# First layer's input of a two-layer attention and gated-unit kernel: transposes moved from TensorE to transfers, the norm in one ScalarE operation, maxima started later

## The chip, the cores and the metric

The kernel runs on one core of one Trainium2 chip. The metric is the device time of the whole program in microseconds (us), the median of several runs. The core's engines each work through their own instruction stream in order and wait for each other by semaphores: TensorE (PE in the profile, its weight loads PEld), VectorE (DVE), ScalarE (ACT), GpSimd (POOL) and SyncE (SP), which here only issues transfers. A queue is an engine's stream of issued transfers; SPq is that of SyncE.

## The reference

Two layers, each an attention block with one shared key and value head and a gated unit behind it. Sizes: 2048 positions, width 448, 16 query heads of 28, hidden width 1792.

```python
def _A_ref(x, wq, wk, wv, wo):                # x: (1, 2048, 448)
    q = (x @ wq) -> (1, 16, 2048, 28)
    k = x @ wk                                # (1, 2048, 28), one head for all
    v = x @ wv
    p = softmax(q @ k.T * 28 ** -0.5)
    return (p @ v -> (1, 2048, 448)) @ wo
def _B_ref(x, w_gate, w_up, w_down):
    return (sigmoid(x @ w_gate) * (x @ w_up)) @ w_down

for _ in range(2):                            # both layers use the same weights
    x = x + _A_ref(layernorm(x), wq, wk, wv, wo)
    x = x + _B_ref(layernorm(x), w_gate, w_up, w_down)
```

## The kernel before

The positions are cut in 16 tiles of 128 rows. Every matrix product takes its f32 operands as a high and a low f16 part. The program has a start (the input of the first layer), then for each layer a main loop of 16 query tiles times 16 key tiles ("steps"), with the gated unit of earlier tiles and other work filled in between.

**The start.** For each tile of x: load (`load_x0`, SP), statistics on VectorE and the inverse deviation on GpSimd (`s0`, `rstd`, L295 to L300, in groups of two or four tiles), the norm and the split in high and low parts (`s1` with `ln_split` and `hilo`: VectorE subtracts and multiplies, L314; ScalarE casts the high part, L306; GpSimd subtracts for the low part, L307 and L308), seven 128x128 transposes on TensorE and their copy to `XT0` by ScalarE (`s2` with `t7`, L320 and L322), the products with the key and value weights (`s3` with `kv`, L337) and the parts of the keys (`build`, L364 to L370), and two transposes of the keys on TensorE with a copy into `KK` (`s4` with `kvt`, L376 to L380). The tile `hl` that holds high and low parts has two buffers, `ktl` (the keys' parts) two. The four stages run staggered in one loop, tile i - 4 in `s1`, i - 6 in `s2`, i - 7 in `s3`, i - 8 in `s4`. Weights are prepared beside it: `prep_kv`, `prep_q`, and `prep_b` for the output projection (`ro`, `WO`) and the gated unit (`rmax` pieces are loaded and squared for a scale).

Projections of the queries (`qproj`, 16 groups of 11 matmuls, four for each block of 512 queries) are generators that a filler (`fill.slice(ns)`) advances by an estimated time. From iteration `SM` on, `first_mx` also makes one of the 16 groups of maxima for the first query tile (`mx_gen`: four matmuls of queries and keys, L472, and four reductions on VectorE, L476). A softmax step of a tile can only start when all 16 groups of that tile are made, reduced, transposed (`fin`, L491) and written into `QS`.

**The main loop.** For each step the order is written out: `ORDER = "FSFSFSFSPXM"`, four scores with an exp each (S: L502, L505), fill slices between (F: query projections first, then the gated unit), the value products of the step before (P: L513), preparation and stages of earlier tiles (X), one group of maxima of the next query tile (M). `paced` advances `prep_b` by step along `PLAN`; the fill rate is the work left over the steps left, with the query projections due by step 48.

Transfers are issued in program order on their engine, and each takes one of eight semaphores in turn, so an issue waits until the transfer eight places before it has landed.

Of the kernel before, what the change touches and what calls it, by code (L numbers as in the profile page):

```python
# [19 lines left out]
def interleaved_layers_kernel(ctx: ExitStack, tc: tile.TileContext, x, wq, wk, wv, wo, wg, wu, wd, out, layers=2):  # L20
# [134 lines left out]
    def prep_q():  # L155
        parts = wk1.tile([128, 4], F32, name="parts", bufs=1)
        for c in range(4):
            junk = wk1.tile([128, D], F32, tag="P", name="junq", bufs=8)
            squares(parts[:, c:c + 1], rq[:, c], junk)
# [106 lines left out]
    PLAN = [(0, 18), (24, 33), (30, 37), (63, 65), (71, 73)]  # L266
# [26 lines left out]
    def rstd(mv, r, n):  # L293
# [6 lines left out]
        nc.gpsimd.tensor_tensor(w, y, z, op=OP.mult)  # L300
        return [(mv[:, i, 0:1], w[:, i:i + 1]) for i in range(n)]
# [14 lines left out]

    def t7(hl, XT, t, ev=nc.vector.tensor_copy):
        p = fps([128, 7, 128], F16, "t7")
        for c in range(7):
            nc.tensor.transpose(p[:, c], hl[:, c], id16)  # L320
            yield C128
        defer(lambda: ev(XT[:, :, t * 128:(t + 1) * 128], p))  # L322
# [21 lines left out]
    ktl = [cst.tile([128, 8, 32], F16, name=f"ktl{i}") for i in range(2)]  # L344
# [11 lines left out]
    def kv(l, XT, t, kt, start=False):  # L356
# [3 lines left out]
        kt_ = ktl[kt % 2]  # L360

        def build():
            if start:
                nc.scalar.activation(kt_[:, 0, 0:28], p[:, 0:28], AF.Copy, scale=2.0 ** -18)  # L364
            else:
                nc.vector.tensor_scalar(kt_[:, 0, 0:28], p[:, 0:28], 2.0 ** -18, None, op0=OP.mult)
            nc.scalar.activation(VV[l][:, kt, 0:28], p[:, 28:56], AF.Copy, scale=2.0 ** -16)
            nc.vector.scalar_tensor_tensor(kt_[:, 1, 0:28], p[:, 0:28], 2.0 ** -18, kt_[:, 0, 0:28],
                                           op0=OP.mult, op1=OP.subtract)
            nc.vector.tensor_copy(kt_[:, 2:8, 0:28], kt_[:, 0:1, 0:28].to_broadcast([128, 6, 28]))  # L370
        defer(build)

    def kvt(l, kt, ev=nc.vector.tensor_copy):
        p = fps([128, 2, 128], F16, "kvt")
        k = ktl[kt % 2].rearrange("p a d -> p (a d)")
        nc.tensor.transpose(p[:, 0], k[:, 0:128], id16)  # L376
        nc.tensor.transpose(p[:, 1], k[:, 128:256], id16)
        yield 2 * C128

        defer(lambda: ev(KK[l][:, :, kt * 128:(kt + 1) * 128], p))  # L380
# [159 lines left out]
    class Block:  # L540
# [143 lines left out]
        def down(self, t, hs):  # L684
# [35 lines left out]
            def dd():  # L720
                if u == 3:
                    fill.gens.insert(0, [qgen(l + 1, 0), G * QCH])
                yield from kv(l + 1, v["XT"], u % 4, u, True)

            def de():
                kt = u
                nc.sync.dma_start_transpose(KK[l + 1][:, :, kt * 128:(kt + 1) * 128],
                                            ktl[kt % 2].rearrange("p a d -> p (a d)"))
                return
                yield  # L730
# [53 lines left out]
    def load_x0(i):  # L784
        xr0[i] = wk1.tile([128, D], F32, tag="h", name="xr0", bufs=HB)
# [16 lines left out]
    def s0(i):  # L802
# [7 lines left out]
        if i in last:  # L810
            n = i + 1 - mvr["a"]
            for j, t in enumerate(rstd(mvr["m"], mvr["r"], n)):
                ls0[mvr["a"] + j] = t
        return
        yield

    def s1(i):
        hl0[i] = ln_split(xr0[i], *ls0[i], nc.gpsimd, xr0[i], nc.scalar.copy)
        if i + HB < NT:
            load_x0(i + HB)  # L820
        return
        yield

    def s2(i):
        flush()
        yield from t7(hl0[i], XT0[i // 4], i % 4, nc.scalar.copy)
        flush()

    def s3(i):
        yield from kv(0, XT0[i // 4], i % 4, i, True)  # L830
        flush()

    def s4(i):
        yield from kvt(0, i, nc.scalar.copy)
# [145 lines left out]
```

## Time and profile before

| | us |
|---|---|
| median of three runs | 2366.12 (2365.82 to 2366.45) |
| the profiled execution's own time | 2366.16 |
| its span, first to last instruction | 2364.4 |
| first exp of the main loop | 106.80 after the span's start |
| mean granted TensorE clock | 0.985 |

Times in the profile count from the span's start; the profiled execution's own time has 1.76 us around the span. In a row of the timeline stand the start, the duration, the engine, the line, the operation, output <- input, their shapes, the count of merged instructions, and in brackets the idle time before and what ended it. In a row of a stretch stand the busy time and the number of instructions of each engine, the granted clock, the share of the transfer engines and GB/s. Line numbers are those of the kernel before.

### The profile page before, as it was taken

To read this page: it belongs to the slowest core of one execution; us is meant where nothing else is said; L and a number is where in the kernel's file an instruction comes from. 1 tells how busy PE (TensorE), PEld (TensorE's weight loads), DVE (VectorE), ACT (ScalarE), POOL (GpSimd) and SP (SyncE) were. 2 spreads that over 40 slices of the span, in tenths; PEclk is the share of its full clock that TensorE was granted. 3 is DMA by queue.
4 is the path that set the end of the run, shared out by engine and by line. 5 is a ranking of instruction groups with operands and counts; after the bars stand their busy time and mean duration, and the time that the engine had idled before them with its cause. 6 is when DMAs were issued, how large, how long until landed. Compare 5 with 4: busy or idle time off the path is not lost.

```text
span 2364.4 us, 41202 instructions
## 1 busy us (share of the span) xinstructions
PE 2239.7 (95%) x15736; PEld 1002.3 (42%) x15736; DVE 1636.2 (69%) x2909; ACT 1562.9 (66%) x2598; POOL 342.0 (14%) x606
## 2 busy tenths in 40 slices
PE   5798899999999999999998999999999999999999
PEld 2222244444444444444572224444444444444456
DVE  6788787777667777773358877767677777777321
ACT  5587777677667676777413777767676776767751
POOL 5203664001110100101001011000000000000010
PEclk9799999999999999999998999999999999999999
DMA  3333563323223232322342113322231313223133
GB/s 113 108 100 92 183 197 103 91 72 94 86 64 97 78 90 72 94 91 73 99 140 53 27 49 91 87 73 83 65 103 58 96 56 102 76 82 94 57 113 116
DMA packets 208071, 213.88 MB, mean 90 GB/s; under 512 B 139952, under 2 KB 168304, under 8 KB 207872
## 3 DMA queue, kind: packets, MB, share of 16 engines
q1 hardware_dynamic: 202496, 196.36, 28.5%
q0 software_dynamic: 5376, 14.87, 1.8%
q8 instruction: 123, 2.02, 0.4%
q14 instruction: 76, 0.62, 0.1%
HBM read 175.37 MB, written 23.59 MB: 84 GB/s over the span
## 4 chain that ended last, share of the span: by engine, by line
PE 51%; DVE 5%; DMA 1%; ACT 1%; issue 0%; SPq 0%; POOL 0%; ACTq 0%; DVEq 0%; POOLq 0%
PE pv L513 12%; PE s L502 10%; PE dn L694 8%; PE gp L337 7%; PE up L337 7%; DVE mp L476 4%; PE mx L472 4%; PE wo L604 2%; PE qp L337 1%; ACT P L505 0%; DMA sums<-rc 0%; DMA KK<-ktl 0%; DVE st L289 0%; DMA XT<-hl 0%; SPq L582 0%
## 5 line engine op out<-in xcount | busy, mean ns | idle before, releaser
L505 ACT ACTIVATE P<-s,esc 128x512 f32<-128x512 f32 x2048 | 1308.6, 688 | 517.1 <-PE s L502 500.2
L476 DVE TENSOR_REDUCE mp<-mx 128x1 f32<-128x512 f32 x2048 | 1268.2, 682 | 410.1 <-PE mx L472 406.1
L502 PE MATMUL s<-QS,KK 96*128 96x512 f16 x2048 | 762.0, 381 | 53.8 <-DVE mp L476 35.0
L337 PEld LDWEIGHTS <-wgu 128*128 128x128 f16 x4928 | 458.7, 98 | 243.7 <-issue 96.4
L513 PE MATMUL pv<-P,VV 128*32 128x512 f32 x4096 | 547.4, 607 | 0.0
L337 PE MATMUL up<-XT,wgu 128*128 128x256 f16 x2464 | 375.8, 273 | 0.6 <-DVE mp L476 0.6
L337 PE MATMUL gp<-XT,wgu 128*128 128x256 f16 x2464 | 375.2, 274 | 0.2
L694 PE MATMUL dn<-WD,h 128*128 128x448 f16 x1344 | 321.7, 352 | 0.0
L502 PEld LDWEIGHTS <-KK 96*128 96x128 f16 x2048 | 194.7, 97 | 171.8 <-issue 94.1
L472 PE MATMUL mx<-KK,QH 32*128 32x512 f16 x2048 | 222.1, 391 | 21.2 <-ACT QH L394 4.8
L472 PEld LDWEIGHTS <-QH 32*128 32x128 f16 x2048 | 53.6, 91 | 395.5 <-issue 377.0
L694 PEld LDWEIGHTS <-h 128*128 128x128 f16 x1344 | 124.1, 98 | 135.8 <-issue 22.0
L513 PEld LDWEIGHTS pv<-P,VV 128*32 128x32 f32 x4096 | 80.9, 108 | 202.9 <-issue 191.0
L587 POOL TENSOR_TENSOR lb<-pvs,lb 128x512 f32<-128x512 f32 x32 | 40.7, 1270 | 786.1 <-DMA lb<-sums 612.8
L668 ACT ACTIVATE h<-th 128x512 f16<-128x512 f32 x112 | 70.2, 627 | 85.0 <-DVE th L665 84.9
L337 PE MATMUL qp<-XT,WQ 128*128 128x512 f16 x352 | 114.9, 403 | 3.8 <-DVE mp L476 2.4
L665 DVE SCALAR_TENSOR_TENSOR th<-th,up 128x512 f32<-128x512 f32 x112 | 76.0, 679 | 59.2 <-PE up L337 46.7
L295 POOL TENSOR_SCALAR rs<-mv 128x1 f32<-128x1 f32 (+2 forms) x53 | 13.6, 257 | 695.5 <-DVE mv L290 693.5
L669 DVE SCALAR_TENSOR_TENSOR h<-th,h 128x512 f16<-128x512 f32 x112 | 78.1, 697 | 46.0 <-ACT h L668 46.0
L657 ACT ACTIVATE th<-gp,gsc 128x512 f32<-128x512 f32 x112 | 76.9, 687 | 48.0 <-PE gp L337 48.0
L604 PE MATMUL wo<-WO,oT 128*128 128x448 f16 x384 | 78.3, 353 | 0.2 <-DVE oT L594 0.2
L337 PEld LDWEIGHTS <-WQ 128*128 128x128 f16 x352 | 33.9, 101 | 67.4 <-issue 43.2
(124 smaller groups left out, 835.6 us busy)
## 6 DMA issues: line engine op xcount, KB each, us to landing
wgu<-wgu_d SPq DMA_DIRECT2D x224, 512.0 KB
QS<-qd SPq DMA_DIRECT2D x384, 32.0 KB
lb<-sums SPq DMA_DIRECT2D x128, 64.0 KB
xr<-in_A_x_dram SPq DMA_DIRECT2D x32, 224.0 KB
qd<-qst POOLq DMA_DIRECT2D x28, 256.0 KB, 2.8
wgu_d<-sgu POOLq DMA_DIRECT2D x14, 512.0 KB, 3.7
QH<-qd SPq DMA_DIRECT2D x28, 128.0 KB
x2d<-x SPq DMA_DIRECT2D x16, 224.0 KB
```

The costliest lines, as they stand in the source:

```text
L337: nc.tensor.matmul(ps, a, b, start=n == 0, stop=n == 10)
L472: nc.tensor.matmul(ps[h], qh[32 * h:32 * h + 32, g], KK[l][32 * h:32 * h + 32, 1, kb * 512:(kb + 1) * 512], start=True, stop=True, tile_po ...
L476: nc.vector.tensor_reduce(mp[:, g, h, kb:kb + 1], ps[h], axis=AX.X, op=OP.max)
L502: nc.tensor.matmul(s, KK[l][0:96, 0, kt * 128:(kt + 1) * 128], QS[l, u][:, g].rearrange("p h n -> p (h n)"), start=True, stop=True)
L505: nc.scalar.activation(p, s, AF.Exp, scale=esc)
L513: nc.tensor.matmul(v[32 * g:32 * g + 32], VV[l][:, kt], P[g], start=kt == 0, stop=kt == KT - 1, tile_position=(0, 32 * g))
L604: nc.tensor.matmul(p, v["oT"][:, a, h * 128:(h + 1) * 128], WO[:, c, h], start=n == 0, stop=n == 11)
L657: defer(lambda: nc.scalar.activation(th, gp.rearrange("p j n -> p (j n)"), AF.Tanh, scale=gsc))
L665: nc.vector.scalar_tensor_tensor(t, th, 1.0, up.rearrange("p j n -> p (j n)"), op0=OP.add, op1=OP.mult)
L668: nc.scalar.activation(h[:, 0], t, AF.Copy, scale=2.0 ** -17)
L669: defer(lambda: nc.vector.scalar_tensor_tensor(h[:, 1], t, 2.0 ** -17, h[:, 0], op0=OP.mult, op1=OP.subtract), 1)
L694: nc.tensor.matmul(p, hs[f // 2][:, a, o:o + 128], WD[:, f, c], start=n == 0, stop=n == 3 * FC - 1)
```

## The change

All in the start, but for `kv` and `kvt`, which the second layer uses too:

- The seven TensorE transposes of each tile and the two of its keys go; transfers with transpose from SP (`t7_dma`, `kvt`) take their place. `s2` is gone, and the stages stand at i - 3, i - 6 and i - 7.
- The norm is one ScalarE operation with a scale and a bias for each row; `rstd` makes the bias with two more GpSimd operations.
- The keys' high part is written seven times by one ScalarE operation with a broadcast input instead of once by ScalarE and six times by a VectorE copy; `ktl` has three buffers. The squares of wq are two operations instead of four.
- All 16 tiles of x are loaded at the start from SP, and the loads of wk and wq are issued from ScalarE's queue. The statistics of a tile are made earlier in the order.
- The maxima begin at iteration 13 with 0.6 of a group per iteration instead of one per iteration from 12 on; the rest follow in a loop of their own, beside 0.6 of a group of the query projection each (0.4 before). All steps of `prep_b` move into that loop; the plan gives 13 of them to the start instead of 18.

```diff
     def prep_q():
-        parts = wk1.tile([128, 4], F32, name="parts", bufs=1)
-        for c in range(4):
+        parts = wk1.tile([128, 2], F32, name="parts", bufs=1)
+        for c in range(2):
...
-    PLAN = [(0, 18), (24, 33), (30, 37), (63, 65), (71, 73)]
+    PLAN = [(0, 13), (24, 33), (30, 37), (63, 65), (71, 73)]
...
-    def rstd(mv, r, n):
+    def rstd(mv, r, n, bias=False):
...
+        if bias:
+            nc.gpsimd.tensor_tensor(z, mv[:, :n, 0], w, op=OP.mult)
+            nc.gpsimd.tensor_scalar(z, z, -1.0, None, op0=OP.mult)
+            return [(z[:, i:i + 1], w[:, i:i + 1]) for i in range(n)]
...
-    def t7(hl, XT, t, ev=nc.vector.tensor_copy):
-        p = fps([128, 7, 128], F16, "t7")
-        for c in range(7):
-            nc.tensor.transpose(p[:, c], hl[:, c], id16)
-            yield C128
-        defer(lambda: ev(XT[:, :, t * 128:(t + 1) * 128], p))
...
         def build():
-            if start:
-                nc.scalar.activation(kt_[:, 0, 0:28], p[:, 0:28], AF.Copy, scale=2.0 ** -18)
...
+            nc.scalar.activation(kt_[:, 1:8, 0:28], p[:, None, 0:28].to_broadcast([128, 7, 28]), AF.Copy, scale=2.0 ** -18)
             nc.scalar.activation(VV[l][:, kt, 0:28], p[:, 28:56], AF.Copy, scale=2.0 ** -16)
...
-            nc.vector.tensor_copy(kt_[:, 2:8, 0:28], kt_[:, 0:1, 0:28].to_broadcast([128, 6, 28]))
...
+    def kvt(l, kt):
+        nc.sync.dma_start_transpose(KK[l][:, :, kt * 128:(kt + 1) * 128], ktl[kt % 3].rearrange("p a d -> p (a d)"))
...
-    for i in range(HB):
+    for i in range(NT):
         load_x0(i)
         if i == 1:
-            load4(rkv[:, 0], wk)
+            load4(rkv[:, 0], wk, nc.scalar)
             load4(rkv[:, 1], wv, nc.gpsimd)
-        if i == 3:
-            load4(rq, wq)
+            load4(rq, wq, nc.scalar)
...
     def s1(i):
-        hl0[i] = ln_split(xr0[i], *ls0[i], nc.gpsimd, xr0[i], nc.scalar.copy)
...
+        b, r = ls0[i]
+        nc.scalar.activation(xr0[i], xr0[i], AF.Identity, bias=b, scale=r)
+        t7_dma(hilo(xr0[i], nc.gpsimd), XT0[i // 4], i % 4)
...
-    L1, L2, L3, L4 = 4, 6, 7, 8
-    st0 = [(L4, s4), (L3, s3), (L2, s2), (L1, s1)]
+    L1, L3, L4 = 3, 6, 7
+    st0 = [(L4, s4), (L3, s3), (L1, s1)]
...
+    nmx, nst, credit = 0, 0, 0.0
+    SQ, SM, RM = 11, 13, 0.6
+    A0, A0E = 0.5, 0.6
...
     for i in range(NT + L4):
...
-        while nst < min(NT, i + 1 + min(max(i - 3, 0), LEAD)):
+        while nst < min(NT, 2 + 3 * i // 2):
...
         if i >= SM:
-            first_mx()
-            nmx += 1
+            credit += RM
+            if credit >= 1 and mx_ready(0, nmx):
+                first_mx()
+                nmx += 1
+                credit -= 1
     for b in range(1, NB):
         fill.add(qgen(0, b), G * QCH)
-    A0E = 0.4
+    k = 0
     while nmx < 4 * NB:
         fill.slice(A0E * QCH)
         first_mx()
         nmx += 1
+        for _ in range(1 + (1 < k < 5)):
+            next(prep[0])
+            prepd[0] += 1
+        k += 1
```

More of the change, by code (lines that the diff above doesn't have):

```diff
@@ L155, in prep_q @@
     def prep_q():
-        parts = wk1.tile([128, 4], F32, name="parts", bufs=1)
-        for c in range(4):
-            junk = wk1.tile([128, D], F32, tag="P", name="junq", bufs=8)
-            squares(parts[:, c:c + 1], rq[:, c], junk)
+        parts = wk1.tile([128, 2], F32, name="parts", bufs=1)
+        for c in range(2):
+            junk = wk1.tile([128, 2, D], F32, tag="x1", name="junq")
+            squares(parts[:, c:c + 1], rq[:, 2 * c:2 * c + 2], junk)
         nc.vector.tensor_reduce(mxa[:, 2:3], parts, axis=AX.X, op=OP.add)
@@ L343, in interleaved_layers_kernel @@
     x2d = drm.tile([NT, 128, D], F32, name="x2d")
-    ktl = [cst.tile([128, 8, 32], F16, name=f"ktl{i}") for i in range(2)]
+    ktl = [cst.tile([128, 8, 32], F16, name=f"ktl{i}") for i in range(3)]
     for t in ktl:
@@ L722, in dd @@
                     fill.gens.insert(0, [qgen(l + 1, 0), G * QCH])
[L723 removed]
+                yield from kv(l + 1, v["XT"], u % 4, u)
             def de():
[L726 to L728 removed]
+                kvt(l + 1, u)
                 return
```

71 lines of the change are left out of this document (20 added, 51 removed).

## The prediction

> **What bounds the kernel now.** I read the granted clock and the busy times of stretches first, then the timeline of the first 140 us, then the waits around the joint of start and main loop.
>
> ```profile
> 41.00:80.00 39.00, 28.77 (x248) 15.31 (x248) 32.11 (x79) 24.25 (x60) 19.57 (x30) 0.68 0.25 73
> 80.00:94.00 14.00, 12.06 (x49) 3.45 (x46) 14.00 (x24) 7.89 (x17) 4.44 (x4) 0.90 0.53 154
> 94.00:107.00 13.00, 6.28 (x19) 2.17 (x20) 4.68 (x12) 3.38 (x9) 2.04 (x3) 0.61 0.55 172
> ```
>
> After the length stand PE, PEld, DVE, ACT and POOL. From 80 to 94 VectorE is full, from 94 to 107 nothing is. The timeline says what these stretches are.
>
> ```profile
> 21.54 0.67 PE L337 MATMUL kv<-WKV,XT 128*128 128x56 f16 x11
> ...
> 76.85 0.72 PE L337 MATMUL kv<-WKV,XT 128*128 128x56 f16 x11
> 82.12 12.04 DVE L476 TENSOR_REDUCE mp<-mx 128x1 f32<-128x512 f32 x20
> 100.49 0.17 DVE L486 TENSOR_SCALAR m<-m 128x16 f16<-128x16 f32 x1
> 101.47 4.87 PE L337 MATMUL qp<-XT,WQ 128*128 128x512 f16 x11
> 106.14 1.26 PE L502 MATMUL s<-QS,KK 96*128 96x512 f16 x4
> 106.80 2.42 ACT L505 ACTIVATE P<-s,esc 128x512 f32<-128x512 f32 x4 [2.75 <-PE s L502]
> ```
>
> The 16 tiles' key products run from 21.5 to 77.6. The last reduction of the maxima ends at 94.15, the maxima are joined only at 100.5, the first exp comes at 106.80. The 64 reductions cost 12.04/20 = 0.60 us each, so a group 2.41 (2.48 where one stands alone, below), and 16 groups 39. The chain that sets 106.80 is: tiles, then maxima on VectorE, then this joint. The joint's waits:
>
> ```profile
> DVE qst L404 <- ACT qst L394: 5.3, 1, 5.3
> ```
>
> VectorE waited 5.3 us for a ScalarE copy, and in ScalarE's order that copy stood behind squares of weights whose loads were still under way.
>
> **The change, part by part: when the tiles come.** ScalarE now issues the loads of wk and wq itself. Each issue waits for the transfer eight places before it, as SP's does here for wq:
>
> ```profile
> SPq L786 <- DMA rq<-in_A_wq_dram: 2.6, 2, 2.4
> ```
> ```profile
> 3.79 0.63 DVE L808 BATCH_NORM_STATS2 st<-xr 128x6 f32<-128x448 f32 x1 [1.54 <-DMA xr<-in_A_x_dram]
> 5.46 0.23 POOL L295 TENSOR_SCALAR rs<-mv 128x2 f32<-128x2 f32 x1 [1.97 <-DVE mv L809]
> 6.23 0.30 ACT L109 ACTIVATE junk<-rkv 128x112 f32<-128x112 f32 x1
> 7.57 0.70 POOL L117 TENSOR_TENSOR pwa<-pwa,half 128x2 f32<-128x2 f32 x1
> ```
> ```profile
> 12.00:14.00 2.00, 0.28 (x3) 0.01 (x1) 1.26 (x3) 0.00 (x0) 0.00 (x0) 1.00 1.04 376
> ```
>
> In the changed program's order these are x tiles 6, 7 and 9 for wk and 11, 12 and 13 for wq. Behind the waiting issues stands everything that ScalarE computes. A tile of 224 KB at 376 GB/s takes 0.6 us, tile 0 is there at 3.8, so tile 13 at 11.6; ScalarE is free at 12.2. Two squares of 0.30, the ones-matmul and VectorE's read of it end near 14.1. VectorE's order holds the statistics of tile 3 behind that read (to 15.0), and GpSimd's holds their `rstd` (5.46 to 7.57 is 2.1 for six operations; eight are 2.8) and the root for the key weights (0.70) ahead of tile 0's low part: that starts at 18.5 (15.0 + 2.8 + 0.7).
>
> ```profile
> L308 POOL TENSOR_TENSOR hl<-xr,hl 128x384 f16<-128x384 f32 x16 | 15.0, 936 | 0.0
> L307 POOL TENSOR_TENSOR hl<-xr,hl 128x64 f16<-128x64 f32 x16 | 5.4, 337 | 24.9 <-ACT hl L306 22.9 <-PE kvt L377 1.9
> ```
> ```profile
> 8.64 0.56 ACT L306 CAST hl<-xr 128x448 f16<-128x448 f32 x1 [2.02 <-DVE xr L314]
> 16.49 0.24 POOL L295 TENSOR_SCALAR rs<-mv 128x4 f32<-128x4 f32 x1
> 18.84 0.20 POOL L300 TENSOR_TENSOR rs<-rs 128x4 f32<-128x4 f32 x1
> 24.47 0.93 PE L320 MATMUL t<-id,hl 128*128 128x128 f16 x7
> 25.44 0.91 ACT L322 COPY XT<-t 128x896 f16<-128x896 f16 x1 [0.47 <-PE t L320]
> ```
> ```profile
> 1202.35 2.96 DMA XT<-hl
> 1258.86 5.64 DMA KK<-ktl
> ```
> ```profile
> L325 SPq DMA_TRANSPOSE XT<-hl x48: 1221/1278/3031, 204.0 to 2300.8; - x48
> L727 SPq DMA_TRANSPOSE KK<-ktl x16: 1168/1186/1904, 442.2 to 1258.9; - x16
> ```
>
> The transfers with transpose that the second layer has already give the price: SP's queue is held 1.28 us by one of a tile, 1.19 by one of keys, and the chain saw a tile land 2.96 after its issue. Low part 0.94 + 0.34 = 1.27: tile 0 lands at 18.5 + 1.27 + 2.96 = 22.7, its key product starts at 22.7 instead of 21.5.
>
> From there a loop sets the pace: `hl` has two buffers, so tile i + 2 is cast only when tile i's transfer has landed. Cast 0.56, low part 1.27, transfer 2.96, hops 0.1: 4.9 for two tiles. TensorE's seven transposes and the two copies (0.93 and 0.91, and less for the keys) leave, as does VectorE's norm; none of them is in this loop. What stands in front in it: the second and third `rstd` of four tiles on GpSimd (16.49 to 19.04 is 2.55 for six operations, 3.4 for eight), of which I count 2.0 each since a pair waits for part of it anyway, and in three pairs a key transfer of 1.19 on SP ahead of a tile's: 4.0 + 3.6 = 7.6. Tile 14 lands at 22.7 + 7 x 4.9 + 7.6 = 64.6, tile 15 half a pair later at 67.0. The last key product ends at 67.5 (77.6 before), its low part at 68.2. The norm on ScalarE is taken as the cast, 0.56; between pairs ScalarE has room for it. Bounds: 7.6 less if all that stands in front fits into waits; with the 5.64 of the keys' row for the 2.96 in half of the seven pairs, 9.4 more.
>
> **The maxima behind them.** In the changed order four groups are ahead of the last tile's key product and twelve behind. Twelve are 12 x 2.48 = 29.8. Beside them VectorE has the output projection's scale and low parts:
>
> ```profile
> L130 DVE SCALAR_TENSOR_TENSOR WO<-ro,swb,WO 128x448 f16<-128x448 f32 x2 | 1.3, 673 | 0.0
> ```
> ```profile
> 43.05 3.38 SPq L218 DMA_DIRECT2D ro<-in_A_wo_dram  x8
> 58.97 0.95 ACT L109 ACTIVATE juno<-ro 128x896 f32<-128x896 f32 x1
> ```
>
> That is 1.3 and six operations of 0.1 to 0.2, 2.3 together. `ro` was issued 16 us before its squares; now it comes after the last key transfer (69.4), takes 3.4 to issue, some 2.4 to land (an estimate, as the x tiles: 3.79 less 0.73 with a shorter queue) and two squares of 0.95, so its sum is there at 77.1, while VectorE reaches that place at 75.6: 1.5 of wait. With 0.6 for the first low part and 1.0 for matmuls at half clock, waits are 3.0. The granted clock was 0.68 from 41 to 80, where TensorE had gaps, and a group of the query projection takes 4.87 at half and 2.55 at full clock, so the first groups behind the gaps are slow. The Trainium skill (TensorE: Matmul & The Clock Gate, Part 1) says that the clock halves after an idle window of about 3.4 us and comes back after a busy one of that length; by it this term would be 1.7 rather than 1.0.
>
> Sum: 68.2 + 29.8 + 2.3 + 3.0 = 103.3, against 94.15. The joint then loses its 5.3 us: loads of `rmax` are one per group of maxima, not two. What is late next is the query's low part (0.7, as the low part above), the join (0.4), and the way through the transposed maxima, which took 100.49 to 106.14, 5.65, with eleven matmuls at half clock in it; at full clock they are 2.3 less, so I take 3.9 with bounds 3.3 and 5.65. First score 108.3, first exp 108.9: 2.1 later.
>
> **What the main loop gets.** Eight groups of query projections and seven matmuls are done ahead of it, against 40 matmuls before: 55 fewer, 12.8 us of TensorE at full clock, and five fewer low parts. And 14 steps of preparation instead of 18: four squares more in the first 24 steps.
>
> ```profile
> 91.38 2.55 PE L337 MATMUL qp<-XT,WQ 128*128 128x512 f16 x11
> 118.25 0.87 ACT L109 ACTIVATE rmax<-rmax 128x784 f32<-128x784 f32 x1
> 119.09 2.44 ACT L505 ACTIVATE P<-s,esc 128x512 f32<-128x512 f32 x4
> 121.37 0.90 ACT L109 ACTIVATE rmax<-rmax 128x784 f32<-128x784 f32 x1
> 131.09 2.48 DVE L476 TENSOR_REDUCE mp<-mx 128x1 f32<-128x512 f32 x4 [1.83 <-PE mx L472]
> 134.00 2.48 DVE L476 TENSOR_REDUCE mp<-mx 128x1 f32<-128x512 f32 x4 [0.42 <-PE mx L472]
> ```
>
> A step with a square is 3.12 (118.25 to 121.37) with ScalarE full: fewer matmuls give nothing there. A step without is 2.91, VectorE 2.48 and 0.42 of waiting for TensorE: that 0.42 is all they can give. Four steps go from 2.91 to 3.12: +0.8. The five of the first 24 without a square gain 0.1 each: -0.5. Five low parts of queries, each as long as one of the output projection's (673 ns), most in gaps: -1.0 (bounds 0 and -3.4). Steps 24 to 48: 24 x 0.42 = 10 at most, a quarter of it: -2.5, because the gaps there also hold splits of the weights. Together -3.2, bounds +0.8 and -12.8. The keys' part in the second layer trades 0.2 of VectorE for some 0.1 of ScalarE per tile, hidden beside the fill.
>
> Total +2.1 - 3.2 = -1.1 on the profiled execution's 2366.16 (span 2364.4); the median is 0.04 below that: 2365.0.
>
> **The rivals.** *Faster:* what I put in front of the transfers fits into waits, the pairs keep 4.9, tile 15 lands at 59.4 and the first exp is at 101.3, 5.5 earlier; with the main loop's -3.2 that is -8.7, 2357.4. For it: SP needs 1.28 + 1.19 = 2.47 a tile, just the 2.45 of the pace. Against: three queues in order (SP, GpSimd, ScalarE) meet in the loop, and each late one delays the others.
>
> *Slower:* the way by transfers is longer than TensorE's and lies in the loop of two buffers. On TensorE a tile took 0.93 and its copy 0.91, 1.84; the transfer takes 2.96, at its worst for keys 5.64. If half the pairs see the worse price, tile 15 lands 9.4 later, the first exp is at 118.3, and with -3.2 the sum is +8.3, 2374.5. It decides from 5.8 us on, 0.8 a pair. For it: transfers of tiles and keys follow each other within 1.3 us here, and an issue took up to 3.03. The Trainium skill (VectorE: DVE Perf Modes, Rules for kernel authors) has TensorE for a 128x128 transpose where the result may go to PSUM, and 1309 ns by transfer against 390. By that figure, seven in a row, an estimate would be 9.2 us a tile; the 2.96 for all seven does not bear this out.
>
> *The change does nothing:* the first exp stays within 1 us and ScalarE sets the steps, 2366.
>
> **How the numbers follow.** About 0.2%, 4.7 us, is what a measurement of this kernel can tell from no change. My forecast and the case of nothing stay inside it: 0.33 and 0.05. Faster 0.34, slower 0.28 (0.01 of it for the page's rule). The likeliest one's own range is 2361.5 to 2370.8; with the other two to their centres and a little beyond, 2354 to 2375 leaves out about 2 in 10.
>
> **What would show it.** Right: ScalarE's first square near 12 to 13, the first tile's key product near 23, transfers of tiles in pairs about 5.9 apart, the last key product near 67, the last reduction near 103, no wait for squares behind it, the first exp near 109, steps with a square still 3.1. Wrong: the first exp before 104 or after 114, or steps without a square below 2.6.

## The result, and the profile after

| | before | changed |
|---|---|---|
| median, us (runs) | 2365.24 (8) | 2373.4 (8) |
| range, us | 2363.29 to 2368.5 | 2371.08 to 2375.39 |
| ratio, 95% interval | | 1.0034 (1.0023 to 1.0045) |
| profiled execution, span | 2364.4 | 2370.5 |
| first exp of the main loop | 106.80 | 116.91 |

The changed kernel is slower by 0.34%, 8.2 us. The forecast was 2365.0, no change. All rows and first exps, here and below, come from one profiled execution of each version, and its time can lie some us from the median: for runs 1, 2, 5 and 14 it is 3.2 to 5.5 above it, for runs 10 and 11 it is 2.7 and 3.3 below, for the others within 2.2. Stretches of the changed kernel, with the columns of the prediction's first fence (PE, PEld, DVE, ACT, POOL, clock, share of the transfer engines, GB/s):

```profile
41.00:80.00 39.00, 25.29 (x200) 10.81 (x198) 18.80 (x42) 18.97 (x51) 20.06 (x32) 0.87 0.57 119
80.00:94.00 14.00, 9.60 (x45) 3.25 (x44) 11.35 (x24) 6.50 (x13) 6.75 (x7) 0.95 0.50 145
94.00:107.00 13.00, 9.19 (x38) 2.63 (x37) 9.65 (x17) 6.26 (x14) 7.53 (x8) 0.79 0.47 150
```

From 41 to 80 VectorE now works 18.80 of 39 us (32.11 before): the norm and the early maxima are gone from there. From 94 to 107, where VectorE had been done, it works 9.65: the maxima have moved behind the tiles. The timeline of the changed kernel, from the first key product to the first exp:

```profile
24.11 0.69 PE L334 MATMUL kv<-WKV,XT 128*128 128x56 f16 x11 [8.74 <-DMA XT<-hl]
...
72.04 0.69 PE L334 MATMUL kv<-WKV,XT 128*128 128x56 f16 x11 [1.55 <-DMA XT<-hl]
...
74.35 0.19 DVE L361 SCALAR_TENSOR_TENSOR ktl<-kv,ktl 128x28 f16<-128x28 f32 x1 [3.18 <-ACT VV L360]
74.45 7.26 DVE L462 TENSOR_REDUCE mp<-mx 128x1 f32<-128x512 f32 x12
...
103.49 1.89 DVE L462 TENSOR_REDUCE mp<-mx 128x1 f32<-128x512 f32 x3 [2.17 <-PE mx L458]
106.56 2.48 DVE L462 TENSOR_REDUCE mp<-mx 128x1 f32<-128x512 f32 x4 [1.18 <-PE mx L458]
109.41 2.48 DVE L462 TENSOR_REDUCE mp<-mx 128x1 f32<-128x512 f32 x4 [0.36 <-PE mx L458]
113.40 0.17 DVE L472 TENSOR_SCALAR m<-m 128x16 f16<-128x16 f32 x1
116.49 1.03 PE L488 MATMUL s<-QS,KK 96*128 96x512 f16 x4
116.91 3.58 ACT L491 ACTIVATE P<-s,esc 128x512 f32<-128x512 f32 x6 [1.08 <-PE s L488]
```

The first key product comes at 24.11 (21.54 before), the last ends at 72.73 (77.57), the last reduction at 111.89 (94.15), the first exp at 116.91, 10.1 later. The way from the last reduction to it is 5.0 instead of 12.65. Of the waits behind the last tile (engine that waits, engine or transfer that it waits for, us in total, times, longest) these three matter:

```profile
ACT qst L380 <- DMA qd<-qst: 5.0, 1, 5.0
...
PE mx L458 <- ACT qf L383: 3.3, 1, 3.3
...
DVE mxb L225 <- ACT juno L109: 2.0, 1, 2.0
```

ScalarE waits 5.0 until the buffer of a query projection has been written out, TensorE waits for ScalarE, and VectorE for TensorE (the 2.17 above). The third is VectorE's wait for the squares of the output projection. The chain that ends in the first wait (start, duration, engine and line) runs through GpSimd:

```profile
90.50 1.42 POOL ro L135
...
93.01 1.81 POOL ro L135
...
94.90 1.04 POOL WO L136
95.94 1.12 POOL qst L388
...
97.35 4.28 DMA qd<-qst
```

GpSimd splits its share of the output projection's weights (L135, L136) from 90.50 to 95.94, and only then makes the projection's low part (L388); the write is issued at 97.35 and lands at 101.63.

### The profile page after: what moved, and what is told of

Read it like the earlier page. It is cut to its first block, busy times and chain, and to the rows that moved or that the text cites. A ratio compares the mean times of both kernels' runs of the same rounds, so it can differ in the third digit from the quotient of the medians.

```text
span 2370.5 us, 40937 instructions
## 1 busy us (share of the span) xinstructions
PE 2226.5 (94%) x15592; PEld 990.3 (42%) x15592; DVE 1624.5 (69%) x2858; ACT 1560.6 (66%) x2583; POOL 348.7 (15%) x621
## 4 chain that ended last, share of the span: by engine, by line
PE 78%; DVE 11%; ACT 3%; DMA 2%; issue 2%; SPq 1%; POOL 0%; ACTq 0%; DVEq 0%; POOLq 0%
PE pv L499 19%; PE s L488 16%; PE dn L680 11%; PE gp L334 10%; PE up L334 10%; DVE mp L462 8%; PE mx L458 6%; PE wo L590 3%; ACT P L491 2%; PE qp L334 2%; DVE st L289 0%; DMA qd<-qst 0%; DMA sums<-rc 0%; DMA lb<-sums 0%; DMA XT<-hl 0%
## 5 line engine op out<-in xcount | busy, mean ns | idle before, releaser
L334 PE MATMUL qp<-XT,WQ 128*128 128x512 f16 x352 | 108.7, 409 | 2.5 <-DVE mp L462 1.2
```

The lines of the kernel that those rows point to most:

```text
L334: nc.tensor.matmul(ps, a, b, start=n == 0, stop=n == 10)
```

## The experiments

The labels number the runs. "First exp" is from the profiled execution of each, the ratio from the timed runs against the kernel before. The diffs are shortened: a comment or a bracketed remark in them can stand for lines that are left out. "Half clock" is the state in which a group of 11 projection matmuls takes 4.87 us instead of 2.55.

**Run 1, four buffers for a tile's parts.**

```diff
-        hl = wk1.tile([128, 7, 128], F16, name="hl", bufs=2)
+        tag = ("hl", "hl", "oT", "oT")[n % 4]    # start only
+        hl = wk1.tile([128, 7, 128], F16, tag=tag, name="hl", bufs=2)
```

> The changed kernel with four buffers instead of two for a tile's high and low parts in the start (two of them in space that the start does not use). Theory A (the loop of two buffers, cast, low part, transfer, sets the pace of the tiles, 6.3 us a pair): the pace falls to what GpSimd needs, about 1.3 us of low part a tile and the inverse deviations, or what SP needs, 2.5 a tile; the last key product ends near 62 to 64 instead of 72.7, and the first exp comes 8 to 10 us earlier, near 108. Theory B (the pace is set by the order in which ScalarE, GpSimd and SP pass each tile on, not by the buffers): the last key product moves by less than 3 us, the first exp stays at 114 to 117, the time stays within 3 us of the changed kernel's.

First exp 117.61, ratio 1.0032 (1.0019 to 1.0045).

```profile
69.19 0.69 PE L338 MATMUL kv<-WKV,XT 128*128 128x56 f16 x11 [1.83 <-DMA XT<-hl]
```

The last key product ends at 69.88, 2.9 earlier, as theory B has it; the first exp gains nothing (117.61 is just beyond B's 117): behind the last tile ScalarE waits 5.3 for the projections' buffer, and seven matmuls at half clock take 3.1 where the changed kernel has most of them at 1.7. This profile is of an execution 5.4 above its median, so part of that may be its own; the ratio of the timed runs shows none of theory A's 8 to 10 us either. The loop of two buffers does not set the pace alone.

**Run 2, maxima earlier.**

```diff
-    SQ, SM, RM = 11, 13, 0.6
+    SQ, SM, RM = 11, 11, 1.0
```

> The changed kernel with the maxima begun at iteration 11 with one group per iteration, instead of at 13 with 0.6: about five groups are behind the last key product instead of twelve. Theory C (the start ends late because twelve groups of 2.48 us are left behind the last tile, while VectorE was busy for 21 of the 49 us before it): seven groups fewer are 17 us; the last reduction ends near 95 to 100 instead of 111.9, the first exp near 100 to 105, the time 10 to 16 us under the changed kernel's 2373, so below the kernel before. Rival D (the earlier groups and the query projections they need stand in TensorE's and ScalarE's order ahead of the tiles and hold them up by as much): the last key product ends 10 us later, near 83, and the first exp stays at 113 to 118.

First exp 102.59, 14.3 earlier, but ratio 1.0039 (1.0026 to 1.0052). ScalarE's timeline:

```profile
102.59 2.42 ACT L491 ACTIVATE P<-s,esc 128x512 f32<-128x512 f32 x4 [1.04 <-PE s L488]
...
110.57 0.86 ACT L109 ACTIVATE rmax<-rmax 128x784 f32<-128x784 f32 x1 [2.22 <-DMA rmax<-in_B_w_gate_dram]
...
115.75 2.40 ACT L491 ACTIVATE P<-s,esc 128x512 f32<-128x512 f32 x4
```

Theory C was right on the first exp and wrong on the time, which it put 10 to 16 us under the changed kernel's. The loop behind the tiles is shorter by those groups and does fewer steps of preparation, and `paced` makes up for them all in the first step: 13 us from its first exp to the next step's. The first tile takes 69.19 instead of 53.82.

**Run 3, three buffers for the projections' parts.**

```diff
-            q = wk1.tile([128, 2, 512], F16, name="qst")
+            tag = ("qst", "qst", "pvs")[n % 3]       # start only
+            q = wk1.tile([128, 2, 512], F16, tag=tag, name="qst", ...)
```

> The changed kernel with three buffers instead of two for the query projections' parts in the start (the third in space that the start does not use). Theory E (the stall at 99 to 107, where ScalarE waited 5.0 us for a buffer until its write had landed, TensorE 3.3 us behind ScalarE and VectorE 2.2 and 1.2 behind TensorE, costs the first exp what VectorE waited): the first exp comes 3 to 4 us earlier, near 113, and the time falls by as much. Rival F (the write is late because writes and loads share the transfers there, and the next buffer would wait for the same, or the matmuls at half clock fill the gap): the first exp moves by less than 1 us.

First exp 115.63, 1.3 earlier and so between E and F, ratio 1.0024 (1.0015 to 1.0033), whose interval overlaps the changed kernel's. VectorE's stalls there are gone:

```profile
95.08 14.44 DVE L464 TENSOR_REDUCE mp<-mx 128x1 f32<-128x512 f32 x24
```

The last reduction ends 2.4 earlier; 1.1 of it is lost again in a longer way to the first exp.

**Run 4, the tiles' transposes back on TensorE.**

```diff
-        t7_dma(hilo(xr0[i], nc.gpsimd), XT0[i // 4], i % 4)
+        hl0[i] = hilo(xr0[i], nc.gpsimd)
+    def s2(i):                                       # at i - 5
+        t7(hl0[i], XT0[i // 4], i % 4, nc.scalar.copy)
```

> The changed kernel with the tiles' seven transposes back on TensorE and their copy on ScalarE, one stage behind the norm; the keys' transposes stay with transfers. Theory G (the transfer's way of 3.1 us against TensorE's 1.84 sits in the loop of two buffers): each pair is 1.3 us shorter, the last key product ends near 64 instead of 72.7, the first exp near 108. Rival H (the way of the transposes does not set the pace; ScalarE's order does, and it has 0.9 us more per tile): the last key product ends at 73 or up to 14 us later, and the first exp is at 117 or later.

Last key product 71.68, first exp 116.90, ratio 1.0035 (1.0022 to 1.0047): the same as with transfers. Rival H, but for a last key product 1.1 earlier. This is the one edit that exchanges the way of the tiles' transposes and little else (one more stage in the loop goes with it), and that way is not what costs here.

**Runs 5 and 6, the changed tiles with the maxima early: preparation as in the kernel before, or spread.** In run 6 one step of preparation stands beside each of the first 13 groups, with the buffers of runs 1 and 3.

```diff
-    SQ, SM, RM = 11, 13, 0.6
+    SQ, SM, RM = 11, 11, 1.0
     def first_mx():
+        for _ in range(1 if nmx == 0 else (nmx > 3) + (nmx > 10)):   # run 6: range(nmx < 13)
+            next(prep[0])
```

> The changed kernel's tiles (transfers, norm on ScalarE, keys' parts in one write), with the second half of the start ordered as in the kernel before: maxima from iteration 11 with one group each, preparation beside the groups with 18 steps, 0.4 of a group of projections in the rest. Run 2 had its first exp at 102.6 but lost 15.4 us in its first tile, where the preparation that it had not done was caught up in one stretch. Theory I (the loss is in the order of the maxima and the preparation, the tiles by transfers themselves gain): the first exp comes at 100 to 104, the first tile takes 55 as before, and with the 2.8 us that the changed kernel gave back in the main loop the time is 5 to 10 us below the kernel before, 2356 to 2360. Rival J (preparation between the tiles fills ScalarE's and SP's order, so the tiles come later by what it takes; or squares wait for loads ahead of the joint as in the kernel before): the first exp is at 106 to 110 and the time 2363 to 2367.

> The changed kernel with maxima from iteration 11, one of the 13 steps of preparation beside each of the first 13 groups, four buffers for a tile's parts and three for the projections' parts. If the order of maxima and preparation made the loss and neither blocks the tiles, the first exp comes at 97 to 102, the first tile takes 54 to 55, and the time is 2352 to 2358, below both kernels. If preparation between the tiles holds them up, the last key product ends at 75 or later, the first exp is at 104 to 108, and the time 2359 to 2366. If the bound is the total work of start and first tiles together (ScalarE's and TensorE's), whatever comes ahead lengthens tiles 0 to 2 by as much, and the time is 2366 to 2372.

Run 5: first exp 115.56, ratio 1.0024 (1.0014 to 1.0035). Run 6: 106.05, 1.0004 (0.9996 to 1.0013). Waits of run 5, then of run 6:

```profile
DVE qst L390 <- ACT qst L380: 6.7, 1, 6.7
ACT ktl L359 <- DMA KK<-ktl: 6.3, 1, 6.3
```

```profile
ACT rmax L109 <- DMA rmax<-in_B_w_gate_dram: 13.7, 3, 10.4
...
DVE ktl L365 <- ACT VV L364: 7.7, 1, 7.7
```

Theory I falls, and run 5 is worse than J. Run 6 is its second case by the last key product (76.59) and the first exp, and its median of 2366.66 lies at the start of the third case: its first three tiles take 177.55 where the kernel before takes 173.71. SP's queue now holds transfers that the keys wait for; with the maxima early, the twelve loads of `QS` stand ahead of the last of them (5.80 us to issue in both runs), and the loads of weight pieces stand behind. What waits for either stands in ScalarE's order ahead of the last tile's keys.

One comparison more: run 2, with the maxima early and no preparation beside them, ends its last key product at 74.37, 1.6 behind the changed kernel's; run 5, with both, at 79.06, 6.3 behind. Of what holds up the tiles there, the larger part goes with the preparation.

**Run 7, the keys' one write alone, in the kernel before.**

```diff
-            if start: ... (one copy on ScalarE or VectorE)
+            nc.scalar.activation(kt_[:, 1:8, 0:28], p[:, None, 0:28].to_broadcast([128, 7, 28]), ...)
...
-            nc.vector.tensor_copy(kt_[:, 2:8, 0:28], kt_[:, 0:1, 0:28].to_broadcast([128, 6, 28]))
```

> The kernel before with one part of the change: the keys' high part in one ScalarE write with a broadcast input, three buffers for it; transposes, norm and order stay as before. Theory K (what the changed kernel gave back behind its first exp, 2.8 us, comes from the second layer's fill, where VectorE wrote the keys' high parts): tiles 15 and 16 take 1.5 to 3 us less together, the first exp stays at 106 to 107, and the time is 1.5 to 3 us below the kernel before. Rival L (it comes from the query projections done ahead and the fewer squares): tiles 15 and 16 take within 0.7 us of before, and the time is within 1 us of it.

First exp 104.81, ratio 0.9985 (0.9974 to 0.9995): this part gains 0.15%, and the profile shows the gain in the start (2.0 at the first exp, 1.2 in the first three tiles). Tiles 15 and 16 take 2.6 more together; theory K falls, and L's condition does not hold either.

**Runs 8 and 9, the order mended, with transfers and with TensorE.** Run 9 is run 7 with only the preparation's lines of this diff (first load at iteration 10).

```diff
+        if i == 9:
+            next(prep[0])
...
     def first_mx():
+        next(prep[0])                       # one step beside every group, 17 in all
...
+        # two pieces' loads issued among the output projection's splits
-                    if kb * 4 + g == 7:
+                    if kb * 4 + g == (12 if l + u == 0 else 7):
                         load_qs(l, u)
```

> The changed kernel with the order mended: maxima from iteration 11, one step of preparation beside every group (17 in all, the output projection's load at iteration 9), the first two loads of weight pieces issued ahead of the output projection's splits, the twelve loads of QS behind the last keys' transfers instead of among them, four buffers for a tile's parts and three for the projections'. In run 6 ScalarE waited 10.4 us for such a load, which stood in SP's order behind the loads of QS, and the last tile's keys stood behind that. Theory M (with these waits gone the tiles by transfers are worth their time): the last key product at 74 to 76, the last reduction at 89 to 93, the first exp at 94 to 98, the first three tiles 174 to 176, the time 2353 to 2358. Rival N (SP's queue is full with two transfers a tile, and each load put between them delays a tile): the last key product at 78 or later, the first exp at 100 to 106, the time 2359 to 2366.

> The kernel before, with transposes on TensorE, and of the change only the keys' one write; preparation as in run 8: its first load at iteration 10, one step beside every group, 17 in all, two loads of weight pieces ahead. The joint's 5.4 us of VectorE behind a ScalarE copy (run 7: last reduction 93.0, first exp 104.8) should go: first exp at 98 to 100, first three tiles 173 to 175, the time 2357 to 2360. If run 8's transfers carry a gain of their own, run 8 is 3 us or more below this one; if the way of the transposes does not matter, both are within 2 us; if transfers cost, this one is lower. If the joint's wait stays because the squares still wait for loads, the first exp stays at 104 to 106 and the time at 2361 to 2364.

Run 8: last key product 76.27, first exp 102.00, ratio 0.9970 (0.9958 to 0.9982). Run 9: 78.67, 100.05, 0.9964 (0.9952 to 0.9976). Run 8 lies between M and N, its time within M's; run 9 is at the edge of its figures. Both beat both kernels, and between these two no difference can be told; they differ in the way of the transposes, but also in the norm, the loads and the buffers. The prediction for the joint holds here: in run 9 VectorE's 5.4 us wait behind the squares is gone.

**Run 10, the order alone, in the kernel before.**

```diff
-    PLAN = [(0, 18), ...
+    PLAN = [(0, 13), ...
-        if i >= SM:
-            first_mx()
+        if i >= SM + 2:
+            credit += 0.6                   # and on, as in the change
...
-    A0E = 0.4
+    A0E = 0.6                               # all steps of prep_b in this loop
```

> The kernel before, tiles as they are, with only the order of the change's second half: 0.6 of a group of maxima per iteration from two iterations later on, the rest in a loop of their own with 0.6 of a group of projections and all steps of preparation, 13 instead of 18. Theory O (this order alone is the loss, whichever way the tiles take): last key product near 73 to 76, then eleven to twelve groups and the stalls of the changed kernel, first exp at 115 to 119, the time 4 to 9 us above the kernel before. Rival P (the loss needs the tiles by transfers, whose keys come late; TensorE's tiles leave VectorE busier before, so the order matters little): first exp at 106 to 111, the time within 2 us of the kernel before.

First exp 109.56, ratio 1.0015 (1.0006 to 1.0023).

```profile
66.30 0.70 PE L337 MATMUL kv<-WKV,XT 128*128 128x56 f16 x11 [0.52 <-ACT XT L322]
```

The run that says most. With all but four groups of maxima and all of that preparation out of its way TensorE's own path ends the last key product at 67.00, 10.6 ahead of the kernel before and 5.7 ahead of the changed kernel's 72.73. The order alone gives more than the 4.8 us that the changed kernel has over the kernel before at this place; the rest of the change takes some of it back. Behind it stand twelve groups instead of six and a half: to the last reduction it is 37.9 instead of 16.6, and from there to the first exp 4.7 instead of 12.6. So the order costs 21.3 less 10.6 and 8.0, about 2.8, at the first exp. That lies in rival P's range, but the median is 3.5 above that of the kernel before, outside P's 2 and below O's 4 to 9.

**Runs 11 and 15, from run 10 to the changed kernel.** Run 11 is the changed kernel with the loads on SP; run 15 is run 10 with the norm on ScalarE and the keys' one write.

```diff
-            load4(rkv[:, 0], wk, nc.scalar)
+            load4(rkv[:, 0], wk)
-            load4(rq, wq, nc.scalar)
+        if i == 3:
+            load4(rq, wq)
```

> The changed kernel with the loads of wk and wq issued by SP again, at their places in the kernel before (behind x tiles 1 and 3), so that ScalarE issues none. In run 10 TensorE's tiles began at 21.1 and the last key product ended at 67.0; in the changed kernel they began at 24.1 and ended at 72.7, 5.7 apart, of which 3.0 stand at the first. Theory Q (ScalarE's waiting issues make those 3.0, as the prediction had 1.2 of it): the first key product comes at 21 to 22.5, the last ends at 69.5 to 71, the first exp 2 to 3 us earlier, near 114 to 115, the time 2370 to 2371. Rival R (the chain through GpSimd's inverse deviations, low part and the transfer makes them, whoever issues the loads): the first key product stays at 23.5 to 24.5, the first exp at 116 to 118.

> Run 10 (the kernel before with the changed order of maxima and preparation) with the norm in one ScalarE operation and the keys' one write; all transposes on TensorE, loads on SP. Against run 11 it lacks the transfers with transpose and the earlier loads and statistics. Theory W (the 3.4 us between run 10's first exp at 109.6 and run 11's at 112.9 are the transfers'): first exp at 108 to 110, as in run 10 or 1.4 earlier as between runs 9 and 12. Theory X (they are the norm's 0.76 on ScalarE, which is in a row with the cast and, in this order, with the projections' copies): first exp at 112 to 114.

Run 11: last key product 68.49, first exp 112.94, ratio 1.0022 (1.0013 to 1.0031). Run 15: 69.61, 113.46, 1.0014 (1.0005 to 1.0023). The start of ScalarE and GpSimd in the changed kernel, then in run 11, there with SP:

```profile
13.92 0.30 ACT L109 ACTIVATE junk<-rkv 128x112 f32<-128x112 f32 x1 [11.70 <-DMA rkv<-in_A_wk_dram]
...
16.40 0.23 POOL L295 TENSOR_SCALAR rs<-mv 128x2 f32<-128x2 f32 x1 [8.62 <-DVE mv L795]
...
19.77 0.31 POOL L311 TENSOR_TENSOR hl<-xr,hl 128x64 f16<-128x64 f32 x1
```

```profile
5.77 0.30 ACT L109 ACTIVATE junk<-rkv 128x112 f32<-128x112 f32 x1 [3.55 <-DMA rkv<-in_A_wk_dram]
6.14 8.72 SPq L773 DMA_DIRECT2D xr<-in_A_x_dram  x12
...
11.62 0.31 POOL L311 TENSOR_TENSOR hl<-xr,hl 128x64 f16<-128x64 f32 x1
...
15.19 9.38 SPq L322 DMA_TRANSPOSE XT<-hl  x4
...
20.11 1.41 PE L334 MATMUL kv<-WKV,XT 128*128 128x56 f16 x22 [12.89 <-DMA XT<-hl]
```

Where ScalarE issues the loads, its first square comes 8.2 us later and tile 0's low part as much. The first two key products, together from 20.11 here, come 4.0 earlier, and so does the first exp. The other 4.2 are lost on SP: its queue is still issuing x loads until 14.86, so the transfer starts 2.4 after the low part is done (12.80), and it takes 4.9 to land where the changed kernel's first takes 3.1. Theory Q is right, and its gain in the profile larger than its figures; the median, 2371.44, is 2.0 below the changed kernel's, and the intervals overlap. Runs 8 and 14 below differ by the same edit alone. For the norm, 41 to 80 in run 10 and in run 15:

```profile
41.00:80.00 39.00, 29.90 (x264) 15.01 (x263) 29.57 (x65) 23.35 (x58) 18.82 (x30) 0.78 0.26 78
```

```profile
41.00:80.00 39.00, 29.77 (x274) 14.79 (x275) 21.21 (x46) 30.43 (x71) 19.63 (x32) 0.82 0.23 67
```

VectorE drops by 8.4 us, ScalarE rises by 7.1, and the last key product ends 2.6 later: theory X by its first exp. The keys' one write is in this step too; alone, in run 7, it moved the first exp the other way.

**Run 12, the norm on ScalarE in run 9.**

```diff
-        hl0[i] = ln_split(xr0[i], *ls0[i], nc.gpsimd, xr0[i], nc.scalar.copy)
+        nc.scalar.activation(xr0[i], xr0[i], AF.Identity, bias=b, scale=r)
+        hl0[i] = hilo(xr0[i], nc.gpsimd)
```

> Run 9 (transposes on TensorE, keys in one write, preparation beside every group) with one more part of the change: the norm in one ScalarE operation with scale and bias per row, in place of VectorE's 0.50 a tile. In run 9 VectorE was full from about 68 to 94. Theory S (VectorE is the bound there, ScalarE has room): the 0.5 of about eight tiles behind the first maxima go, the last reduction ends at 89 to 91 instead of 93.7, the first exp is at 95.5 to 97.5, the time 2352 to 2354. Rival T (0.76 and 0.56 in a row on ScalarE lengthen the way of a tile, in a loop of two buffers, by what VectorE gains or more, and two more operations on GpSimd put the first tile later): the last key product ends at 79 or later, the first exp at 100 to 103, the time 2356 to 2360.

First exp 98.65, 1.4 earlier, ratio 0.9964 (0.9950 to 0.9977), no difference in time: the first exp lies between S and T, the time in T's range. With the maxima early, the norm on ScalarE moves the first exp the other way than from run 10 to run 15.

**Run 13, the keys' transposes back on TensorE in run 11** (`kvt` with two transposes and ScalarE's copy, in the first layer).

> Run 11 (the changed kernel with the loads on SP) with the keys' two transposes and their copy back on TensorE and ScalarE in the first layer; the tiles' stay with transfers. Theory U (the 3.4 us left are in the keys' transfers: three buffers for the keys' parts wait for them, 3.0 us at the last tile, and each takes 1.2 us of SP ahead of a tile's transfer): the last key product ends at 65 to 67.5, its low part 1 us behind it instead of 1.8, the first exp at 109 to 110.5, the time 2366 to 2369. Rival V (they are in the tiles' way or in the tail, where stalls move as the start moves): the first exp stays at 112 to 114.

Last key product 73.76, first exp 114.58, ratio 1.0033 (1.0022 to 1.0045). Theory U falls: the keys' transfers are worth 1.6 at the first exp here. The intervals of runs 11 and 13 overlap.

**Runs 14 and 16, the transfers with order and loads mended.** Run 14 is run 8 with run 11's loads; run 16 has `QS` at group 14 instead of 12.

> Run 8 (all transposes by transfers, order mended) with the loads of wk and wq on SP as in run 11. Run 8 had its first exp at 102.0, runs 9 and 12 with TensorE's transposes at 100.05 and 98.65. If the loads are worth 4.0 here too, the first exp is at 98 and the time 2353 to 2355, and the transfers are as good as TensorE or 2 us better. If VectorE, full behind the first maxima, sets the end whatever the first tile does, the first exp stays at 100 to 102 and the time at 2356 to 2358.

> Run 14 with the twelve loads of QS two groups later, behind all loads of weight pieces. In run 14 ScalarE waited 5.6 us for a piece that stood behind them, VectorE 2.9 for ScalarE in the joint, TensorE 4.3 for VectorE, and ran at half clock behind that. If that chain made the way from the last reduction (87.3) to the first exp (97.5), the first exp comes at 92 to 95 and the time is 2 to 4 us under run 14's 2354.1. If the QS loads, 5.6 us to issue, then end the chain themselves, the first exp stays at 96 to 98 and the time at 2353 to 2355.

Run 14: last key product 69.88, first exp 97.49, ratio 0.9940 (0.9926 to 0.9953), as expected if the loads are worth their 4.0 here too: against run 8 the first key product comes 3.8 earlier (20.28 for 24.12) and the median is 3.3 lower. Run 16: 92.65, median 2351.2 (2348.0 to 2353.37), ratio 0.9939 (0.9926 to 0.9951). Run 14's wait at ScalarE and what SP issued ahead of the load; then run 16:

```profile
87.11 0.86 ACT L109 ACTIVATE rmax<-rmax 128x784 f32<-128x784 f32 x1 [5.61 <-DMA rmax<-in_B_w_gate_dram]
```
```profile
77.41 5.64 SPq L426 DMA_DIRECT2D QS<-qd  x12
```
```profile
76.45 9.87 DVE L469 TENSOR_REDUCE mp<-mx 128x1 f32<-128x512 f32 x16 [0.18 <-PE mx L465]
...
92.65 2.42 ACT L498 ACTIVATE P<-s,esc 128x512 f32<-128x512 f32 x4 [2.43 <-PE s L495]
```

Run 16's last reduction ends at 86.32, its first exp 14.2 before that of the kernel before. Its first tile gives back 4.4 (59.62 against 55.22). Its first exp lies in the first case's range; in time it can't be told from run 14. It has the lowest median of all, 14.9 us under the kernel before's median of that comparison.

## Why the prediction was wrong, by its steps

The first exp came 8.0 later than the forecast 108.9. By the terms of the sum: the last keys' low part was done at 74.5 instead of 68.2 (6.3: the first tile 1.4, the pace 3.8, the way from key product to low part 1.1), the waits behind it were 6.3 instead of 3.0, the work between them was 1.0 shorter, and the joint 0.6.

Four steps lead by one edit or a few from the kernel before to the changed one:

| | last key product ends | first exp | step | ratio (interval) |
|---|---|---|---|---|
| before | 77.57 | 106.80 | | 1 |
| + order (run 10) | 67.00 | 109.56 | +2.8 | 1.0015 (1.0006 to 1.0023) |
| + norm on ScalarE, keys' one write (run 15) | 69.61 | 113.46 | +3.9 | 1.0014 (1.0005 to 1.0023) |
| + transfers, earlier loads, statistics and weights (run 11) | 68.49 | 112.94 | -0.5 | 1.0022 (1.0013 to 1.0031) |
| + loads of wk, wq from ScalarE (changed) | 72.73 | 116.91 | +4.0 | 1.0034 (1.0023 to 1.0045) |

The first exps come from one profile each, and those of runs 10 and 11 are of executions quicker than their medians. In the times the steps are less sharp: the order and the whole sum stand out, the norm's 3.9 does not appear, and the intervals of neighbours overlap.

*When the tiles come: the step that failed.* The mechanism of the late first tile was right in every link (ScalarE's issues, the first square, VectorE's statistics, GpSimd's root, the low part), and each link was short: first square 13.92 where ScalarE was to be free at 12.2, low part 19.77 for 18.5, first key product 24.11 for 22.7. I set its price against the kernel before's 21.54 and called it 1.2; run 11 shows that the same tiles start at 20.11 without it, so it was 4.0. The Trainium skill (DMA: Bandwidth & Descriptors, Issuing engines are not separate DMA queues) says that issuing from several engines only saves the time to issue; here SP was spared six issues, 3.1 us in the kernel before, and ScalarE, with its work behind the waiting issues, began 8.2 later.

The pace was to be 5.9 us a pair and was 6.4; the last key product came 5.2 later than forecast. The loop that I built it from, cast, low part and transfer in two buffers, is at most 2.9 of it (run 1). The norm has its own row on ScalarE, not the 0.56 of the cast:

```profile
L803 ACT ACTIVATE xr<-xr,rs 128x448 f32<-128x448 f32 x16 | 12.2, 761 | 0.0
```

"ScalarE has room for it" is what run 15 speaks against in this order: 2.6 later at the last key product, with the keys' one write in the same step.

And the gain was put down to the wrong part. "77.6 before" was read as TensorE's transposes; it was the order, the maxima and the preparation between the tiles. Run 10 ends its last key product at 67.00 with TensorE's transposes untouched, where I forecast 67.5 as the worth of the transfers.

*The maxima behind them.* Twelve groups of 2.48 behind the last tile and 2.3 us of other work were right, together 1.0 too long. The waits were 3.0 in the sum and 6.3 in the trace: 2.0 at the output projection's sum (1.5 forecast), 0.6 at its first low part (0.6), and 3.7 where 1.0 stood for half clock. That is the chain behind the unwritten projection buffer: each early projection is written out by a transfer, the buffers are two, and the write waits for GpSimd, which is at the output projection until 95.94. The sum has VectorE's share of that split and puts GpSimd's and the write at nothing; run 3, with a third buffer, gives 2.4 for it at the last reduction. How much of the write's 4.28 is due to loads of weight pieces beside it was not tried.

*The joint* was right: 5.0 from the last reduction to the first exp (5.6 forecast, 12.65 before). Its wait for squares did not come back.

*The main loop* was to give 3.2 in steps up to 48. The first three tiles took 173.38 for 173.71, 0.3. The span shows 4.0 behind the first exp, but 3.0 of it are in tile 15, with the second layer's start in it, which took from 178.9 to 182.2 in all these runs with no edit that goes with it, and 1.5 of that come back in tile 16; 1.2 are behind the last exp, where the profile of before is the longest of all. So the likely sum is 10.1 less 0.3 and some 1.0 over tiles 3 to 14 (counted from 0), 8.8, beside 8.2 from the medians. Why tile 15 varies was not tried.

*The rivals.* "Slower" gave 2374.5 and a first exp at 118.3, near what came, but by transfers in the loop of two buffers. Runs 1 and 4 take that loop away or put TensorE's transposes into it, and the first exp stays: the number was near and the mechanism wrong. The rule named there, TensorE for 128x128 transposes (the Trainium skill, VectorE: DVE Perf Modes, Rules for kernel authors), is not borne out as a cost: run 4, with the tiles back on TensorE, has 1.0035 beside 1.0034, and run 13, with the keys back, 1.0033 beside run 11's 1.0022. "Faster" did not come: from first to last key product its pairs of 4.9 are in none of the runs; the shortest are 6.0 (run 10) and 6.1 (run 1).

What stays open: which part of -0.5 from run 15 to run 11 belongs to the transfers and which to the earlier loads, statistics and weights, and why the norm's 3.9 at the first exp is not seen in the time. Run 10's profile, 2.7 under its median, may make that step look larger than it is; this was not tried.

## What to carry to other kernels

Before crediting a gain to the operations that are replaced, ask what else the same edit takes out of their way: here the reordered maxima and preparation alone gave the tiles what the transfers were credited with. A load issued from an engine that computes cost that engine the waits of the issue (8.2 us here), and a transfer put in the place of computation waited for what stood ahead of it in its queue (5.8 us of `QS` loads in runs 5 and 6); so look at the order of the queue together with it. When work is taken out of the start, count what it carried along: run 2 gained 14 us at the first exp and lost 15 to preparation that had no place any more.

## What the runs showed of the hardware that was not expected

A transfer with transpose of 128x896 f16 holds SP for 1.24 us (1.28 in the second layer of before), and its tile was there 3.1 after the issue for the changed kernel's first tile, 2.9 for its last, and 4.9 for run 11's first. Two transfers a tile, of keys and tile, still let the last key product end at 69.0 in run 16; with TensorE's transposes the earliest was 67.0, in run 10, with twelve groups of maxima and the preparation behind the tiles. The norm in one ScalarE operation with scale and bias per row takes 761 ns for 128x448, the cast of the same tile 566. A group of 11 matmuls of 128x512 took 4.87 us in the joint of run 14, where TensorE had waited 4.26 us, and 2.55 in run 16, where it had waited 1.36.
